# Six PSUM banks for scores, seven visits of three passes, relu on VectorE: a fused sigmoid attention and ReGLU kernel

## The chip, the cores and the metric

The kernel runs on one core of one Trainium2 chip. The time is device microseconds (us) of one launch; a run's profile gives a span that is some 2 us shorter.

TensorE is called PE, VectorE DVE, ScalarE ACT and GpSimd POOL, as the profile does.

## The reference

```python
# q, k, v: (8, 12, 448, 64)   batch, heads, seq, head_dim
scores = q @ k.T / sqrt(64) - log(448)
attn   = sigmoid(scores)                    # no softmax: no row sum is needed
o      = attn @ v
x      = o.transpose(0, 2, 1, 3).reshape(3584, 768)
gate   = maximum(x @ w_gate, 0)             # w_gate, w_val: (768, 1536)
val    = x @ w_val
out    = (gate * val) @ w_out               # w_out: (1536, 768)
```

## The kernel before

The work of a batch (448 rows) is attention on 12 heads, in three *blocks* of four heads, and then the feed-forward on 768 columns. A block has seven *passes*: a pass makes the scores of 64 key positions for four heads with four 64x64 matmuls, and one sigmoid of 896 columns on ACT. After a block's passes, 28 *value* matmuls make x^T for it, which is copied out of PSUM. (PSUM is where this kernel's matmuls put their results; it is divided into eight banks of 512 fp32 columns, and each is held by a tile from a pool until another engine has copied it out.)

The feed-forward of batch b runs on PE in 128x128 tiling. Into it are put *visits*: short interruptions in 64x64 tiling that do some passes, and sometimes the values, of batch b+1. Only the *opening* (batch 0's attention, some 30 us) has no feed-forward to hide it. Block n is head group n mod 3 of batch n // 3, so blocks 0 to 2 are the opening and blocks 3 to 5 are visited during batch 0's feed-forward.

```python
qkp = tile_pool("qkp", bufs=2, PSUM)        # 2 score tiles [128, 2, 512] fp32: 2 banks each
wkp = tile_pool("wkp", bufs=4, PSUM)        # 4 banks: gate, value, y, x^T, transposes

def scores(n, c):
    ps = qkp.tile([P, 2, 512], FP32)
    for r, h, o, bank in (...):             # four 64x64 quarters
        nc.tensor.matmul(ps[o:o+64, bank, 0:S], kT[...], qT[...], tile_position=(r, o), ...)
    nc.scalar.activation(pt, ps[:, :, 0:S], AF.Sigmoid, bias=bias_t, scale=qk_scale)

def up(b, f):                               # one 128-wide chunk of d_ff
    # 6 matmuls -> gate (wkp), relu on ACT; 6 matmuls -> value (wkp); product on DVE
    nc.scalar.activation(g_sb, acc[:, 0:S], AF.Relu)
    nc.vector.tensor_tensor(hT[f][...], g_sb, ps[1][:, 0:S], op=mult)

def visit():
    i0 = state["pass"]; n, c = divmod(i0, NCH)
    i1 = min(i0 + (3 if c == 0 and n > NBLK else 2), i0 + NCH - c, NPASS)
    for i in range(i0, i1):
        if c == 0 and i == i0 + 2 and n > NBLK:
            values(n - 1, range(NCH))
        scores(*divmod(i, NCH))
    ...                                     # then feed(i): loads, casts, transposes

# [cut]  the opening
for i in range(NP0 + 2):                    # NP0 = 21 passes
    scores(n, c)                            # while i < NP0
    ...                                     # values trail by 4 passes, later by 2
    if c == 1: cast_qk(n + 1, "k", nc.vector); cast_qk(n + 1, "q", nc.vector)
    if c in (3, 5): transposes(n + 1, "k" if c == 3 else "q")
    if 13 <= i < NP0: start_next()          # next load of weights or of a block
```

## Time and profile before

| | before |
|---|---|
| device time, median of 4 runs | 434.88 us (434.75 to 435.08) |
| span of the profiled run | 432.7 us |
| PE busy | 97% |
| sigmoids of the opening | 7.27 to 26.70 us |
| first gate matmul of the second chunk | 29.70 us |
| first gate matmul of batch 1 | 81.14 us |
| first gate matmul of batch 7 | 386.03 us |

The last four rows are marks: the starts of certain instructions in the timeline, in us from the start of the span. Since PE is nearly always busy, the distance of two marks is the time of a stage, and stages add up to the span. Two more rows, from the page's groups (busy us in total, mean ns of one, idle time of the engine ahead of them), show the work that the change moves between engines:

```profile
L232 ACT ACTIVATE gate_sb<-gv_ps 128x448 f32<-128x448 f32 x96 | 52.3, 544 | 91.6 <-PE gv_ps L220 91.6
...
L204 DVE TENSOR_SCALAR xT<-pv_ps 128x448 f16<-128x448 f32 x48 | 27.7, 619 | 127.1 <-PE pv_ps L191 127.1
```

The relu costs ACT 544 ns, and a copy of the same shape costs DVE 619 ns: DVE is the slower of the two for it.

### The profile page before, as it was taken

What the parts mean: (1) busy time and instruction counts of PE and PEld (TensorE: products, weight loads), DVE (VectorE), ACT (ScalarE), POOL (GpSimd) and SP (SyncE); (2) the same over time, 40 slices, a digit from 0 to 9 for tenths busy, and PEclk for the clock granted to TensorE, in tenths of its full rate; (3) what the DMA queues carried; (4) which work ended last, traced back from release to release, by engine and by line L of the source; (5) the groups of instructions that cost most, each with busy time, mean ns of one, the idle gap of its engine ahead of it and who ended that gap; (6) DMA issues with size and microseconds to landing.
All of it is one profiled execution on the core that took longest, in us unless ns stands there. A gap on an engine that the chain in (4) does not pass through costs nothing.

```text
span 432.7 us, 7894 instructions
## 1 busy us (share of the span) xinstructions
PE 421.4 (97%) x3296; PEld 214.6 (50%) x3296; DVE 99.5 (23%) x168; ACT 235.4 (54%) x325; POOL 105.6 (24%) x139
## 2 busy tenths in 40 slices
PE   7789999999999999999999999999999999999996
PEld 3344455544555445544455445554455544455554
DVE  3432332132202222122211233023220232212210
ACT  5955656655556656555546555565555556532221
POOL 2687669222301403113021133013030100000000
PEclk9999999999999999999999999999999999999999
DMA  8999997891238920695217932299114320030014
GB/s 302 385 385 385 388 394 261 229 268 46 42 77 238 300 45 2 172 244 163 42 42 198 251 126 44 53 234 294 22 21 111 79 44 2 17 94 1 2 36 111
DMA packets 62516, 66.52 MB, mean 154 GB/s; under 512 B 33936, under 2 KB 52752, under 8 KB 62480
## 3 DMA queue, kind: packets, MB, share of 16 engines
q1 hardware_dynamic: 61232, 64.17, 50.8%
q10 hardware_dynamic: 1248, 1.84, 1.2%
q8 instruction: 26, 0.43, 0.4%
q14 instruction: 10, 0.08, 0.1%
HBM read 47.19 MB, written 11.01 MB: 134 GB/s over the span
## 4 chain that ended last, share of the span: by engine, by line
PE 86%; DMA 6%; ACT 3%; POOL 2%; issue 1%; DVE 1%; SPq 0%; DVEq 0%; POOLq 0%
PE gv_ps L220 47%; PE y_ps L252 25%; PE qk_ps L167 8%; PE pv_ps L191 6%; DMA st_wo<-in_moe_w_out_dram 5%; ACT PT L177 3%; DMA st_k<-in_k_dram 2%; POOL wo L137 1%; PE tr L153 0%; POOL wg L137 0%; DVE xT L204 0%; SPq L90 0%; DVE h16q L105 0%; POOL v L112 0%; POOL v L114 0%
## 5 line engine op out<-in xcount | busy, mean ns | idle before, releaser
L177 ACT ACTIVATE PT<-qk_ps,bias_t 128x896 f16<-128x896 f32 x168 | 158.1, 1011 | 58.5 <-PE qk_ps L167 58.5
L220 PE MATMUL gv_ps<-xT,wv 128*128 128x448 f16 x576 | 127.8, 353 | 0.0
L220 PE MATMUL gv_ps<-xT,wg 128*128 128x448 f16 x576 | 127.4, 353 | 0.2 <-DVE xT L204 0.2
L252 PE MATMUL y_ps<-wo,hT 128*128 128x512 f16 (+2 forms) x684 | 114.5, 323 | 0.4 <-POOL wo L137 0.4
L232 ACT ACTIVATE gate_sb<-gv_ps 128x448 f32<-128x448 f32 x96 | 52.3, 544 | 91.6 <-PE gv_ps L220 91.6
L235 DVE TENSOR_TENSOR hT<-gate_sb,gv_ps 128x448 f16<-128x448 f32 x96 | 59.6, 621 | 168.1 <-PE gv_ps L220 137.5
L252 PEld LDWEIGHTS <-hT 128*128 128x128 f16 x684 | 64.2, 98 | 48.6 <-issue 8.2
L220 PEld LDWEIGHTS <-wv 128*128 128x128 f16 x576 | 54.6, 98 | 57.3 <-issue 8.6
L220 PEld LDWEIGHTS <-wg 128*128 128x128 f16 x576 | 54.9, 98 | 53.5 <-issue 5.7
L112 POOL CAST v<-st_v 128x448 f16<-128x448 f32 x24 | 13.5, 562 | 180.4 <-PE pv_ps L191 171.1
L204 DVE TENSOR_SCALAR xT<-pv_ps 128x448 f16<-128x448 f32 x48 | 27.7, 619 | 127.1 <-PE pv_ps L191 127.1
L167 PE MATMUL qk_ps<-qT,kT 64*64 64x448 f16 x672 | 51.4, 360 | 4.7 <-ACT PT L177 3.9
L264 ACT ACTIVATE ysb<-y_ps 128x512 f32<-128x512 f32 (+2 forms) x56 | 27.4, 489 | 39.8 <-PE y_ps L252 39.5
L191 PE MATMUL pv_ps<-PT,v 64*64 64x448 f16 x672 | 39.0, 349 | 0.8 <-ACT PT L177 0.8
L167 PEld LDWEIGHTS <-kT 64*64 64x64 f16 x672 | 15.4, 105 | 34.7 <-issue 30.1
L105 POOL CAST h16q<-st_q 128x896 f16<-128x896 f32 x21 | 19.6, 932 | 40.2 <-DMA kT<-h16k 32.8
L191 PEld LDWEIGHTS <-v 64*64 64x64 f16 x672 | 20.0, 107 | 12.6 <-issue 1.8
L105 POOL CAST h16k<-st_k 128x896 f16<-128x896 f32 x21 | 19.6, 932 | 0.4 <-DMA qT<-h16q 0.3
L114 POOL CAST v<-st_v 64x448 f16<-64x448 f32 x24 | 13.7, 570 | 1.0
L113 POOL CAST v<-st_v 64x448 f16<-64x448 f32 x24 | 13.4, 560 | 1.5
L137 POOL CAST wv<-st_wu 128x1536 f16<-128x1536 f32 x6 | 8.8, 1470 | 3.4 <-DMA st_wu<-in_moe_w_val_dram 3.4
L137 POOL CAST wg<-st_wg 128x1536 f16<-128x1536 f32 x6 | 8.8, 1467 | 2.0 <-DMA st_wg<-in_moe_w_gate_dram 1.7
(25 smaller groups left out, 47.9 us busy)
## 6 DMA issues: line engine op xcount, KB each, us to landing
out_dram<-ysb SPq DMA_DIRECT2D x54, 192.0 KB, 2.7
st_q<-in_q_dram SPq DMA_DIRECT2D x23, 448.0 KB, 5.9
st_v<-in_v_dram SPq DMA_DIRECT2D x23, 448.0 KB, 6.6
st_k<-in_k_dram SPq DMA_DIRECT2D x22, 448.0 KB, 5.0
st_wg<-in_moe_w_gate_dram SPq DMA_DIRECT2D x6, 768.0 KB, 12.2
st_wu<-in_moe_w_val_dram SPq DMA_DIRECT2D x6, 768.0 KB, 12.2
st_wo<-in_moe_w_out_dram SPq DMA_DIRECT2D x6, 768.0 KB, 11.4
st_v<-in_v_dram ACTq DMA_DIRECT2D x1, 448.0 KB, 5.4
```

The source lines that it names most:

```text
L105: eng.tensor_copy(o, i)
L114: eng.tensor_copy(t[64:128, 1], st[0:64, 1])
L137: eng.tensor_copy(dst, st[:])
L167: nc.tensor.matmul(ps[o : o + 64, bank, 0:S], kT[r : r + 64, c, h, :], qT[r : r + 64, :, h, :], start=True, stop=True, tile_position=(r, o ...
L177: nc.scalar.activation(pt[:], ps[:, :, 0:S], AF.Sigmoid, bias=bias_t[:], scale=qk_scale)
L191: nc.tensor.matmul(pv[pr][o : o + 64, 0:S], t[r : r + 64, pr, c * D : (c + 1) * D], pt[r : r + 64, pr, :], start=(c == 0), stop=(c == NCH ...
L204: nc.vector.tensor_scalar(out=x[:], in0=pv[pr][:, 0:S], scalar1=XSCALE, scalar2=None, op0=AOP.mult)
L220: nc.tensor.matmul(acc[:, 0:S], w[:, dc, jj * P : (jj + 1) * P], xT[b, dc][:], start=(dc == 0), stop=(dc == NDC - 1),)
L232: nc.scalar.activation(g_sb[:], acc[:, 0:S], AF.Relu)
L235: nc.vector.tensor_tensor(out=hT[f][:, o : o + S], in0=g_sb[:], in1=ps[1][:, 0:S], op=AOP.mult)
L252: nc.tensor.matmul(y[:, 0:w], hT[f][:, o : o + P], wo[f // FG][:, f % FG, c0 : c0 + w], start=(f == 0), stop=(f == NFC - 1),)
L264: nc.scalar.activation(dst, y[:, 0:w], AF.Copy, scale=OUT_SCALE)
```

## The change

The intent: fewer and larger visits. A visit of three passes needs three score tiles, six of the eight banks; the feed-forward is left with two, and so its banks must be freed fast. ACT would be in the way there, since its sigmoids come in threes; so relu and the output copies go to DVE, and the x^T copies to ACT. Block 3's transposes move into the opening, those of blocks 4 and 5 and the values go to score tiles, and those of block 6 to the DMA.

```diff
-    qkp = ... bufs=2, PSUM        wkp = ... bufs=4, PSUM
+    qkp = ... bufs=3, PSUM        wkp = ... bufs=2, PSUM
@@ transposes
+        if n <= NBLK: tr = wkp.tile(...)
+        else:         tr = qkp.tile([P, 2, 512], FP32, tag="qk")[:, 0, 0:S].bitcast(FP16) ...
@@ values
-            PT[n] = [wkp.tile([P, 512], FP32, tag="wk") for _ in range(2)]
+            PT[n] = qkp.tile([P, 2, 512], FP32, tag="qk")
-                nc.vector.tensor_scalar(out=x[:], in0=pv[pr][:, 0:S], scalar1=XSCALE, ... mult)
+                if n >= NBLK or (pr and n == NBLK - 1):
+                    nc.scalar.activation(x[:], pv[:, pr, 0:S], AF.Copy, scale=XSCALE)
+                else:
+                    nc.vector.tensor_scalar(...)
@@ up
-                nc.scalar.activation(g_sb[:], acc[:, 0:S], AF.Relu)
+        nc.vector.tensor_scalar(out=g_sb[:], in0=gate[:, 0:S], scalar1=0.0, ... max)
@@ down
-                if j == 0:                 # output copy on ACT
+                if nb == 2 and j == 0:     # only one of the two last, narrow ones
@@ feed: block m's transposes, while the block before it has its passes
-        if c == 0 and NPRO <= n + 3 < NB: load_all(n + 3)
-        if c == 4 and NPRO < m < NB: dma_transposes(m)
-        if c == 5 and NBLK < m <= NPRO: transposes(m, "k"); transposes(m, "q")
+        if c == 4 and NBLK < m < NPRO: transposes(m, "k"); transposes(m, "q")
+        if c == 3 and NPRO <= m < NB: dma_transposes(m)
+        if c == 3 and NPRO <= m + 1 < NB: load_all(m + 1)
@@ visit
-        i1 = min(i0 + (3 if c == 0 and n > NBLK else 2), i0 + NCH - c, NPASS)
+        i1 = min(i0 + 3, NPASS)            # may run over the end of a block
@@ the opening
-        order = halves("g", 0) + halves("u", 0) + [3] + ...
+        order = halves("g", 0) + [3] + halves("u", 0) + ...
+            if i == 14: cast_qk(NBLK, "k", nc.vector)
+            if i == 15: transposes(NBLK, "k"); cast_qk(NBLK, "q", nc.vector)
+            if i == 16: transposes(NBLK, "q")
+            if i in (18, 21): gv_part(0, 0, wg, [0, 1] if i == 18 else [2, 3])
@@ batches
-                count = 3 * NBLK + (2 if b == 0 else 0)          # 11, then 9
+                count = NBLK * NCH // 3 + (1 if b == 0 else 0)   # 8, then 7
-                if b == 0 and step == 12: transposes(NBLK, "k"); transposes(NBLK, "q")
# [cut: helpers for starting the first chunk's gate and value early, a set of blocks already valued,
#  how many loads are issued first, where batch 0's visits begin]
```

More of the change, by code (lines that the diff above doesn't have):

```diff
@@ L58 @@
     ysbp = ctx.enter_context(tc.tile_pool(name="ysbp", bufs=3))
-    qkp = ctx.enter_context(tc.tile_pool(name="qkp", bufs=2, space=bass.MemoryType.PSUM))
-    wkp = ctx.enter_context(tc.tile_pool(name="wkp", bufs=4, space=bass.MemoryType.PSUM))
+    qkp = ctx.enter_context(tc.tile_pool(name="qkp", bufs=3, space=bass.MemoryType.PSUM))
+    wkp = ctx.enter_context(tc.tile_pool(name="wkp", bufs=2, space=bass.MemoryType.PSUM))
     bias_t = const.tile([P, 1], FP32, name="bias_t")
@@ L150, in transposes @@
         h16 = qk16.pop((nm, n))
-        tr = wkp.tile([P, NCH, 2, KC], FP16, tag="wk", name="tr")
+        if n <= NBLK:
+            tr = wkp.tile([P, NCH, 2, KC], FP16, tag="wk", name="tr")
+        else:
+            tr = qkp.tile([P, 2, 512], FP32, tag="qk", name="tr")[:, 0, 0 : S].bitcast(FP16)
+            tr = tr.rearrange("p (c h k) -> p c h k", c=NCH, h=2)
         for c in range(cut[0], cut[-1]):
@@ L184, in values @@
         if chunks[0] == 0:
-            PT[n] = [wkp.tile([P, 512], FP32, tag="wk", name="pv_ps") for _ in range(2)]
+            PT[n] = qkp.tile([P, 2, 512], FP32, tag="qk", name="pv_ps")
         pv = PT[n]
@@ L191, in values @@
                 nc.tensor.matmul(
-                    pv[pr][o : o + 64, 0:S],
+                    pv[o : o + 64, pr, 0:S],
                     t[r : r + 64, pr, c * D : (c + 1) * D],
@@ L203, in values @@
                 x = xTp.tile([P, S], FP16, tag="xT", name="xT")
-                nc.vector.tensor_scalar(
-                    out=x[:], in0=pv[pr][:, 0:S], scalar1=XSCALE, scalar2=None, op0=AOP.mult
-                )
+                if n >= NBLK or (pr and n == NBLK - 1):
+                    nc.scalar.activation(x[:], pv[:, pr, 0:S], AF.Copy, scale=XSCALE)
+                else:
+                    nc.vector.tensor_scalar(
+                        out=x[:], in0=pv[:, pr, 0:S], scalar1=XSCALE, scalar2=None, op0=AOP.mult
+                    )
                 xT[b, 2 * i + pr] = x
@@ L212, with gv_part, up @@
     MM_US = 0.189
-    def up(b: int, f: int):
-        j, jj = divmod(f, FG)
-        ps = []
-        for w in (wg[j], wv[j]):
-            acc = wkp.tile([P, 512], FP32, tag="wk", name="gv_ps")
-            for dc in range(NDC):
-                nc.tensor.matmul(
-                    acc[:, 0:S],
-                    w[:, dc, jj * P : (jj + 1) * P],
-                    xT[b, dc][:],
-                    start=(dc == 0),
-                    stop=(dc == NDC - 1),
-                )
-                if dc < NDC - 1:
-                    yield MM_US
-            ps.append(acc)
-            if len(ps) == 1:
-                g_sb = gsbp.tile([P, S], FP32, tag="gsb", name="gate_sb")
-                nc.scalar.activation(g_sb[:], acc[:, 0:S], AF.Relu)
+    begun: dict = {}
+    def gv_part(b: int, f: int, w, dcs):
+        key = (b, f, w is wg)
+        if key not in begun:
+            begun[key] = wkp.tile([P, 512], FP32, tag="wk", name="gv_ps")
+        j, jj = divmod(f, FG)
+        for dc in dcs:
+            nc.tensor.matmul(
+                begun[key][:, 0:S],
+                w[j][:, dc, jj * P : (jj + 1) * P],
+                xT[b, dc][:],
+                start=(dc == 0),
+                stop=(dc == NDC - 1),
+            )
+        return begun[key]
+    def up(b: int, f: int, gate_done=0, val_first=0):
+        if val_first:
+            gv_part(b, f, wv, range(val_first))
+        for dc in range(gate_done, NDC):
+            gate = gv_part(b, f, wg, [dc])
+            if dc < NDC - 1:
+                yield MM_US
+        g_sb = gsbp.tile([P, S], FP32, tag="gsb", name="gate_sb")
+        nc.vector.tensor_scalar(out=g_sb[:], in0=gate[:, 0:S], scalar1=0.0, scalar2=None, op0=AOP.max)
+        yield MM_US
+        for dc in range(val_first, NDC):
+            val = gv_part(b, f, wv, [dc])
+            if dc < NDC - 1:
                 yield MM_US
         o = (b % NHALF) * S
-        nc.vector.tensor_tensor(
-            out=hT[f][:, o : o + S], in0=g_sb[:], in1=ps[1][:, 0:S], op=AOP.mult
-        )
+        nc.vector.tensor_tensor(out=hT[f][:, o : o + S], in0=g_sb[:], in1=val[:, 0:S], op=AOP.mult)
         yield MM_US
@@ L280, in ffn @@
         for f in range(NFC):
-            yield from up(b, f)
+            if b == 0 and f == 0:
+                yield from up(b, f, 4, 4)
+            else:
+                yield from up(b, f)
         for col0 in blocks128(b):
@@ L286, in ffn_us @@
         return NFC * 2 * NDC * MM_US + len(blocks128(b)) * NFC * (DM / 2400.0 + 0.004)
-    LOAD_AHEAD = 3
     NPRO = 2 * NBLK
@@ L299, in feed @@
         n, c = divmod(i, NCH)
-        m = n + LOAD_AHEAD
-        if c == 0 and NPRO <= m < NB:
-            load_all(m)
         m = n + 1
@@ L305, in feed @@
             cast_block(m)
-        if c == 4 and NPRO < m < NB:
-            dma_transposes(m)
-        if c == 5 and NBLK < m <= NPRO:
+        if c == 4 and NBLK < m < NPRO:
             transposes(m, "k")
             transposes(m, "q")
+        if c == 3 and NPRO <= m < NB:
+            dma_transposes(m)
+        if c == 3 and NPRO <= m + 1 < NB:
+            load_all(m + 1)
+    valued: set = set()
     state = {"pass": NBLK * NCH}
@@ L315, in visit @@
         i0 = state["pass"]
-        n, c = divmod(i0, NCH)
-        i1 = min(i0 + (3 if c == 0 and n > NBLK else 2), i0 + NCH - c, NPASS)
+        i1 = min(i0 + 3, NPASS)
+        n = i0 // NCH - 1
+        ready = n >= NBLK and n not in valued
         for i in range(i0, i1):
-            if c == 0 and i == i0 + 2 and n > NBLK:
-                values(n - 1, range(NCH))
+            if ready and i == i0 + 2:
+                values(n, range(NCH))
             scores(*divmod(i, NCH))
-        if i0 == NPASS:
-            values(n - 1, range(NCH))
+        if ready and i0 == NPASS:
+            values(n, range(NCH))
+        if ready:
+            valued.add(n)
         for i in range(i0, i1):
@@ L349, in halves @@
             return [(kind, j, 0), (kind, j, 1)]
-        order = halves("g", 0) + halves("u", 0) + [3] + halves("g", 1) + halves("u", 1)
+        order = halves("g", 0) + [3] + halves("u", 0) + halves("g", 1) + halves("u", 1)
         order += [4] + halves("g", 2) + halves("u", 2) + halves("o", 0) + [5]
@@ L358, in start_next @@
                 load_all(what)
-                cast_block(what)
+                if what > NBLK:
+                    cast_block(what)
+                else:
+                    cast_v(what, nc.gpsimd)
             else:
@@ L375 @@
             cast_v(n, nc.gpsimd)
-        for _ in range(4):
+        for _ in range(2):
             start_next()
@@ L398 @@
                 transposes(n + 1, "k" if c == 3 else "q")
-            if 13 <= i < NP0:
+            if i == 14:
+                cast_qk(NBLK, "k", nc.vector)
+            if i == 15:
+                transposes(NBLK, "k")
+                cast_qk(NBLK, "q", nc.vector)
+            if i == 16:
+                transposes(NBLK, "q")
+            if i in (18, 21):
+                gv_part(0, 0, wg, [0, 1] if i == 18 else [2, 3])
+            if 11 <= i < NP0:
                 start_next()
@@ L405 @@
             if b + 1 < B:
-                count = 3 * NBLK + (2 if b == 0 else 0)
-                lo = 4.0 if b == 0 else 0.0
+                count = NBLK * NCH // 3 + (1 if b == 0 else 0)
+                lo = 6.0 if b == 0 else 0.0
                 todo = [lo + (k + 0.5) * (total - lo) / count for k in range(count)]
@@ L411 @@
                 t += cost
-                if b == 0 and step == 12:
-                    transposes(NBLK, "k")
-                    transposes(NBLK, "q")
                 if order and step % 8 == 0:
```

## The prediction

> **What bounds the kernel now.** I read the page first: the busy line, then the 40 slices.
>
> ```profile
> PE 421.4 (97%) x3296; PEld 214.6 (50%) x3296; DVE 99.5 (23%) x168; ACT 235.4 (54%) x325; POOL 105.6 (24%) x139
> ...
> PE   7789999999999999999999999999999999999996
> ```
>
> PE is idle only in the first three slices and the last one. ACT, at 54%, is the next engine. So PE's own work sets the end; a change pays if it takes time out of PE's stream, or shortens the opening. A busy PE still need not be at its peak, so I looked in the timeline at how closely its matmuls follow each other.
>
> ```profile
> 100.37 0.92 PE L220 MATMUL gv_ps<-xT,wg 128*128 128x448 f16 x4
> ...
> 101.22 0.57 PE L167 MATMUL qk_ps<-qT,kT 64*64 64x448 f16 x8
> 101.66 1.91 ACT L177 ACTIVATE PT<-qk_ps,bias_t 128x896 f16<-128x896 f32 x2 [1.68 <-PE qk_ps L167]
> 101.73 0.55 PE L220 MATMUL gv_ps<-xT,wg 128*128 128x448 f16 x2
> ```
>
> Columns: start, duration, engine, line, instruction, count. Elsewhere six 448-wide matmuls start 1.135 us apart as a group (389.44 to 390.57 below), so one is 0.189 us. The four at 100.37 have streamed by 101.13; the feed-forward goes on at 101.73. The visit of two score passes thus takes 0.60 us. Its matmuls need 2 x 448/2.4 GHz = 0.373 us, the four 64x64 quarters running together. **0.23 us of each visit is the switch into and out of the 64x64 tiling.** A visit of three passes and 28 value matmuls (start 94.37; feed-forward from 94.28 to 96.39) takes 2.11 us against 10 x 0.187 = 1.87: 0.24 us again. The price is per visit, not per pass.
>
> Second, the buffers: how close is an evacuation to what PE needs next? In the last batch, which has no visits:
>
> ```profile
> 389.44 1.30 PE L220 MATMUL gv_ps<-xT,wv 128*128 128x448 f16 x6
> ...
> 390.57 1.30 PE L220 MATMUL gv_ps<-xT,wg 128*128 128x448 f16 x6
> 390.85 0.62 DVE L235 TENSOR_TENSOR hT<-gate_sb,gv_ps 128x448 f16<-128x448 f32 x1 [1.65 <-PE gv_ps L220]
> 391.71 1.30 PE L220 MATMUL gv_ps<-xT,wv 128*128 128x448 f16 x6
> ```
>
> The product starts 0.28 us after its group has streamed and ends at 391.47, 0.24 us before PE would want the same bank if there were two.
>
> Third, the opening and batch 0:
>
> ```profile
> 11.32 15.38 ACT L177 ACTIVATE PT<-qk_ps,bias_t 128x896 f16<-128x896 f32 x17 [0.35 <-PE qk_ps L167]
> ```
> ```profile
> 23.59 1.47 POOL L137 CAST wv<-st_wu 128x1536 f16<-128x1536 f32 x1 [0.57 <-DMA st_wu<-in_moe_w_val_dram]
> ...
> 26.09 0.94 POOL L105 CAST h16q<-st_q 128x896 f16<-128x896 f32 x1 [1.02 <-DMA st_q<-in_q_dram]
> ...
> 65.96 1.47 POOL L137 CAST wo<-st_wo 128x1536 f16<-128x1536 f32 x1 [0.51 <-DMA st_wo<-in_moe_w_out_dram]
> ...
> 67.48 1.79 PE L252 MATMUL y_ps<-wo,hT 128*128 128x512 f16 x13 [0.44 <-POOL wo L137]
> ```
>
> From 11.3 to 26.7 us ACT is gapless: 17 sigmoids at 0.905 us set the pace. The DMA moves 385 GB/s in the slices up to about 65 us; POOL casts wait for loads (brackets), and once PE waits 0.44 us for the last of w_out.
>
> **What the Trainium skill says.** "TensorEngine Tiling (Array Packing)", Key Properties: changing the tiling mode drains TensorE. The trace agrees: 0.23 us per visit. "TensorE: Matmul & The Clock Gate", Back-to-back issue gap: N/2.4 + 2.5 ns, for 448 columns 189.2 ns; the trace has 0.189 us. "VectorE: DVE Perf Modes", Mode 2x_2P: that mode needs SBUF, as PSUM has one read port; so I take relu on VectorE at the plain rate, like the present x^T copy (619 ns for 448 columns). "Perfetto Trace Analysis", Matmuls: groups should rotate through PSUM banks so that evacuation overlaps the next group; the change leaves just two for that.
>
> **The change part by part.**
>
> *Visits.* Batch 0 goes from 11 visits to 8, batches 1 to 6 from 9 to 7: 3 + 12 = 15 fewer. Passes and values stay the same. With three score tiles a visit's three passes need not wait for a sigmoid (visits are some 7 us apart, three sigmoids take 2.8). Gain 15 x 0.23 = **3.45 us** (2.76 in batches 1 to 6).
>
> *Relu and output copies to VectorE, x^T to ScalarE.* Neither is on PE's path. VectorE gets 2 x 0.62 us per 2.27 us of gate and value, 55%. What matters is the release: 0.28 + 0.62 us plus about 0.05 for the semaphore (an x^T copy ended at 28.33 and PE started at 28.38) = 0.95 us against 1.135 us until PE returns to that bank. Slack 0.19 us. For outputs: 0.3 + about 0.69 (152 ns + 512/0.96 GHz, estimated from the 619 ns copy) + 0.05 = 1.04 against 12 x 0.109 = 1.31 us. Slack 0.27. So **0**. ScalarE gains 2 x 0.54 us in three visits per batch: hidden.
>
> *Transposes on PE.* The 14 of one block take 0.79 us (42.13 to 42.92). Block 3's move into the ScalarE-paced opening, block 6's go to the DMA: gain **1.6 us**. Those of blocks 4 and 5 stay, but now write score tiles just after three passes have filled all three. The instruction order confirms that both wait for ScalarE. Take V as the start of a visit: sigmoids start at V + 0.44 and each 0.905 later, each lasting some 0.97. Block 4: k^T waits to V + 1.45 instead of 0.65, then q^T to V + 2.35: 1.3 us lost. Block 5's visit has values too: k^T waits 0.35 us and q^T, which takes the values' tile, 0.55 us for the x^T copies on ScalarE: 0.9. Loss **2.2 us**.
>
> *Loads.* Block 6's loads (1.38 MB, 3.6 us at 385 GB/s) move behind w_out, which lands that much earlier: the 0.44 us wait goes, gain **0.44 us**.
>
> *Opening.* Block 3 now loads ahead of w_val's first quarter. From the casts above, q of block 3 lands at about 19.5 + 2 x 1.2 = 21.9 instead of 26.1, and w_val 3.6 us later: its second half at about 27.2, cast by 28.7. PE transposes q of block 3 at pass 16, about 23.4 after the cast, some 1.1 us after pass 17's scores would have gone, so ScalarE's chain ends about 1.1 us later, near 27.9. The four gate matmuls done early, the split x^T copy and four early value matmuls should have won some 1.1 us; they now cover this delay. Gate and value of the first chunk end about together at 29.6, and the next gate waits for relu to about 30.15. Before, it started at 29.70. Loss **0.45 us**.
>
> *Sum.* 3.45 + 1.6 + 0.44 - 2.2 - 0.45 = 2.84 us. I take 3.2, since the early opening steps could hide more than I give them: 434.99 - 3.2 = **431.8 us**.
>
> **The rivals.**
>
> 1. *Two banks are too few.* If VectorE's release is later than I read by more than 0.19 us, PE stalls at nearly all 192 gate and value groups. At 0.05 us each that is 9.6 us and the time about 441. For it: the slack is small, and end times of pipelined matmuls are modelled. Against it: the 0.28 us lag repeats to 0.01 through the last batch, the product's mean of 621 ns holds while POOL works too, and ScalarE's sigmoids no longer delay relu. I give it one chance in ten in some degree.
>
> 2. *DMA transposes come too late.* They are now issued before a block's first pass by a margin of only one visit for some blocks. The pair before, issued at 135.83, released POOL at 140.2 and 141.5: 5.65 us. A gap between visits is at least 5.55 + 0.8 = 6.35 us. At the start of each batch I count k and q landing at 7.7 us and needed at 9.3. If that fails by 1 us in six batches the gain is gone: 438.
>
> 3. *The opening or the loads gain more.* If block 3's data come in time, the ScalarE chain keeps its 26.7 us end and some 1 us more is won; without the transposes' waits another 2.2 us: 428.5. Against it: at 385 GB/s nothing lands sooner, and three tiles are full when the transposes want them.
>
> More than 2% (8.7 us) is nowhere to be found: all visits' switches together were 65 x 0.23 = 15 us, and 50 remain.
>
> **Range and chances.** The visits' gain is firm, from a price that repeats; the other terms nearly cancel and are good to about 2 us. Down to 429.0 if rival 3 comes half true; up to 435.5 for a small stall of rivals 1 or 2. Faster by over 2%: 0.04. Slower by over 2%: 0.05. Within 2%: 0.91.
>
> **What the changed profile would show.** Right: a batch of 50.91 us (half of 84.27 to 186.09, two batches) becomes about 50.45; visits of three passes take about 0.79 us; gate groups still follow at 1.135 us and no wait of gv_ps for relu or product adds up, except in batch 0; tr waits for PT and x^T, some 2 us in total; no wait for w_out; the first chunk ends near 30 us. Wrong: gv_ps waiting for VectorE in every batch (rival 1), qk_ps waiting for kT or qT from the DMA (rival 2), or ScalarE's sigmoids of the opening ending away from 27.9 us. If a visit of three passes cost more than 0.79 us, the price would not be per visit and the main term would fall.

## The result, and the profile after

| | before | after |
|---|---|---|
| median of 4 runs each, us | 434.88 | 433.76 |
| lowest to highest, us | 434.75 to 435.08 | 433.40 to 434.29 |
| ratio after / before | | 0.9975 [0.9957, 0.9992] |

A ratio is the mean time of one kernel's fast runs over that of the other's of the same rounds, so it is not quite the ratio of the medians. The change gained 1.1 us, where 3.2 were forecast. The page of the changed kernel:

```profile
PE 418.7 (97%) x3282; PEld 216.6 (50%) x3282; DVE 165.9 (38%) x276; ACT 178.8 (41%) x217; POOL 102.6 (24%) x137
...
PE   7779899999999999999999999999999999999996
...
L230 PE MATMUL gv_ps<-xT,wg 128*128 128x448 f16 x576 | 128.1, 353 | 0.6 <-DVE gate_sb L247 0.3
...
L247 DVE TENSOR_SCALAR gate_sb<-gv_ps 128x448 f32<-128x448 f32 x96 | 59.9, 624 | 71.9 <-PE gv_ps L230 71.9
```

PE's busy time fell by 2.7 us, yet the span fell by just 0.2. Against the slices before, the third (21.6 to 32.4 us, the opening) and the fifth (43 to 54 us) each lost a tenth: time went missing early. The gate matmuls waited 0.6 us in the whole run, so two banks hardly stall the feed-forward.

The marks put the difference into stages. The predicted column takes the terms of the prediction that belong to a stage; for the rest of batch 0 those are three visits (-0.69), the transposes (-1.6 and +2.2) and w_out (-0.44).

| stage | before, us | after, us | change | predicted |
|---|---|---|---|---|
| start to the second chunk's first gate matmul | 29.70 | 32.17 | +2.47 | +0.45 |
| rest of batch 0 | 51.44 | 50.83 | -0.61 | -0.53 |
| batches 1 to 6 | 304.89 | 302.13 | **-2.76** | -2.76 |
| batch 7 to the end | 46.67 | 47.37 | +0.70 | 0 |
| span | 432.7 | 432.5 | -0.20 | -2.84 |

The profiled run of the changed kernel was its slowest (434.29 us, 0.53 above the median), so its opening is a bad one. In three more profiles of kernels with the same opening, in the experiments below, the first mark lay at 31.32, 31.66 and 32.96 us: the opening lost between 1.6 and 3.3 us. From the medians it is about 1.55: the other stages gained 0.61 + 2.76 - 0.70 = 2.67, and 1.12 arrived. (The other stages hardly vary: where an experiment leaves them alone, its profile has 50.8, 302.1 and 47.4 us for them again.)

**A visit of three passes** in the timeline (columns: start, duration, engine, line, operation, count; all times in us):

```profile
92.88 0.35 PE L230 MATMUL gv_ps<-xT,wg 128*128 128x448 f16 x1
...
93.16 0.76 PE L171 MATMUL qk_ps<-qT,kT 64*64 64x448 f16 x12
...
93.86 1.12 PE L230 MATMUL gv_ps<-xT,wg 128*128 128x448 f16 x5
```

The one gate matmul has streamed (its columns are all in) by 92.88 + 0.189 = 93.07, and the feed-forward goes on at 93.86. The visit takes 0.79 us for 3 x 0.187 us of matmuls: the price is 0.23 us, as it was for two passes.

**The opening's sigmoids** (timeline of ACT; the bracket is the idle time before a row and what ended it):

```profile
7.94 3.70 ACT L181 ACTIVATE PT<-qk_ps,bias_t 128x896 f16<-128x896 f32 x4 [0.49 <-PE qk_ps L171]
11.99 10.93 ACT L181 ACTIVATE PT<-qk_ps,bias_t 128x896 f16<-128x896 f32 x12 [0.35 <-PE qk_ps L171]
23.11 1.01 ACT L181 ACTIVATE PT<-qk_ps,bias_t 128x896 f16<-128x896 f32 x1 [0.19 <-PE qk_ps L171]
24.92 1.01 ACT L181 ACTIVATE PT<-qk_ps,bias_t 128x896 f16<-128x896 f32 x1 [0.81 <-PE qk_ps L171]
26.47 2.90 ACT L181 ACTIVATE PT<-qk_ps,bias_t 128x896 f16<-128x896 f32 x3 [0.54 <-PE qk_ps L171]
...
30.51 0.54 ACT L209 ACTIVATE xT<-pv_ps 128x448 f16<-128x448 f32 x1 [1.14 <-DVE xT L211]
```

Before, 17 sigmoids ran without a gap to 26.70. Now there are three gaps after 22.9 us and the last sigmoid ends at 29.37, 2.67 later. Counted in starts, at 0.905 us from one to the next: 0.67 is there from the first sigmoid on (7.94, before 7.27), the next two gaps delay the chain by 0.26 and 0.90, the last by 0.64. PE's side of the gaps:

```profile
11.07 0.55 PE L157 MATMUL tr<-ident,h16k 128*128 128x128 f16 x7 [1.48 <-DVE kT L163]
...
22.11 0.56 PE L157 MATMUL tr<-ident,h16k 128*128 128x128 f16 x7 [0.37 <-DVE h16k L105]
...
23.93 0.57 PE L157 MATMUL tr<-ident,h16q 128*128 128x128 f16 x7 [0.75 <-DVE h16q L105]
...
25.98 0.38 PE L171 MATMUL qk_ps<-qT,kT 64*64 64x448 f16 x4 [0.60 <-ACT PT L181]
...
32.17 1.29 PE L230 MATMUL gv_ps<-xT,wg 128*128 128x448 f16 x6 [0.34 <-DVE gate_sb L247]
```

Four things are to be seen. At 11.07 PE waits for one of the two feed-forward banks, whose k^T copy stands on DVE behind block 1's casts, which wait for their load. At 22.11 and 23.93 PE takes up block 3's transposes before their casts are done, and the next scores stand behind them. At 25.98 scores wait for a score tile: the values of block 2 hold one of the three. At 32.17 the second chunk's gate waits for the first chunk's relu.

The late start is in part luck. PE's first seven transposes, from 5.43 us, took 0.95 us here and 0.61 before, but between 0.60 and 0.95 from profile to profile of the edited kernels whose transposes start at that moment. Where they took 0.60 (e3_two), the first sigmoid started at 7.48, still 0.21 later than before.

**The end.** The last pair of output tiles, before (first fence) and after:

```profile
423.77 5.29 PE L252 MATMUL y_ps<-wo,hT 128*128 128x256 f16 x47
```
```profile
426.87 0.69 DVE L283 TENSOR_SCALAR ysb<-y_ps 128x512 f32<-128x512 f32 x1 [2.17 <-PE y_ps L269]
427.61 1.45 PE L269 MATMUL y_ps<-wo,hT 128*128 128x128 f16 x23 [0.73 <-DVE ysb L283]
```

The last block's columns 512 to 767 are made as two tiles of 128 columns at once, so with the 512-wide tile three banks are in use. Two exist: PE waits 0.73 us for the 512-wide copy.

### The profile page after: what moved, and what is told of

Same layout as the page of the kernel before. It is cut to its first block, busy times and chain, and to the rows that moved or that the text cites. A ratio compares the mean times of both kernels' runs of the same rounds, so it can differ in the third digit from the quotient of the medians.

```text
span 432.5 us, 7873 instructions
## 1 busy us (share of the span) xinstructions
PE 418.7 (97%) x3282; PEld 216.6 (50%) x3282; DVE 165.9 (38%) x276; ACT 178.8 (41%) x217; POOL 102.6 (24%) x137
## 4 chain that ended last, share of the span: by engine, by line
PE 93%; DMA 3%; ACT 2%; DVE 1%; issue 1%; ACTq 0%
PE gv_ps L230 51%; PE y_ps L269 26%; PE qk_ps L171 8%; PE pv_ps L195 6%; DMA st_k<-in_k_dram 3%; ACT PT L181 2%; PE fill L357 1%; PE tr L157 1%; ACT xT L209 0%; DVE ysb L283 0%; DVE h16k L105 0%; DVE xT L211 0%; DVE gate_sb L247 0%; DVE h16q L105 0%; ACT kT L161 0%
## 5 line engine op out<-in xcount | busy, mean ns | idle before, releaser
L247 DVE TENSOR_SCALAR gate_sb<-gv_ps 128x448 f32<-128x448 f32 x96 | 59.9, 624 | 71.9 <-PE gv_ps L230 71.9
L283 DVE TENSOR_SCALAR ysb<-y_ps 128x512 f32<-128x512 f32 (+2 forms) x56 | 31.1, 556 | 105.7 <-PE y_ps L269 105.7
L105 POOL CAST h16q<-st_q 128x896 f16<-128x896 f32 x20 | 18.6, 930 | 223.2 <-DMA st_q<-in_q_dram 199.5
L171 PE MATMUL qk_ps<-qT,kT 64*64 64x448 f16 x672 | 48.5, 359 | 2.4 <-ACT PT L181 2.1
L171 PEld LDWEIGHTS <-kT 64*64 64x64 f16 x672 | 16.2, 105 | 27.9 <-issue 21.7
L209 ACT ACTIVATE xT<-pv_ps 128x448 f16<-128x448 f32 x43 | 21.0, 547 | 6.0 <-PE pv_ps L195 4.8
L105 POOL CAST h16k<-st_k 128x896 f16<-128x896 f32 x20 | 18.6, 928 | 0.0
```

What stands on the lines that cost most here:

```text
L105: eng.tensor_copy(o, i)
L171: nc.tensor.matmul(ps[o : o + 64, bank, 0:S], kT[r : r + 64, c, h, :], qT[r : r + 64, :, h, :], start=True, stop=True, tile_position=(r, o ...
L209: nc.scalar.activation(x[:], pv[:, pr, 0:S], AF.Copy, scale=XSCALE)
L247: nc.vector.tensor_scalar(out=g_sb[:], in0=gate[:, 0:S], scalar1=0.0, scalar2=None, op0=AOP.max)
L283: nc.vector.tensor_scalar(out=dst, in0=y[:, 0:w], scalar1=OUT_SCALE, scalar2=None, op0=AOP.mult)
```

## The experiments

Each is an edit of the changed kernel. Times are medians; "before" is the kernel before in the same rounds. All are shown with the expectation ahead of the run. All outputs are right. Since "before" itself moves by up to 0.4 us, differences of 0.2 us to the changed kernel mean little.

| run | us (lowest to highest, runs) | ratio to before [95%] |
|---|---|---|
| e1_tail | 433.88 (432.81 to 435.08, 6) | 0.9974 [0.9957, 0.9990] |
| e2_opening | 433.88 (433.70 to 434.68, 5) | 0.9978 [0.9966, 0.9990] |
| e3_two | 438.35 (438.22 to 439.13, 4) | 1.0080 [1.0067, 1.0093] |
| e4_later | 431.78 (431.49 to 432.25, 5) | 0.9929 [0.9916, 0.9941] |
| o1_dve_order | 433.54 (433.47 to 433.68, 4) | 0.9965 [0.9950, 0.9980] |
| o2_values_later | 433.20 (432.56 to 434.56, 4) | 0.9960 [0.9931, 0.9988] |
| o3_opening | 432.06 (431.90 to 432.15, 4) | 0.9930 [0.9915, 0.9945] |
| e6_all | 429.16 (429.07 to 429.26, 4) | 0.9864 [0.9849, 0.9879] |
| e7_relu_scalar | 452.02 (451.57 to 453.05, 4) | 1.0389 [1.0368, 1.0410] |
| e8_four_banks | 464.14 (463.95 to 465.33, 4) | 1.0672 [1.0648, 1.0696] |
| e9_no_split | 434.08 (433.24 to 434.51, 4) | 0.9971 [0.9952, 0.9990] |

My theory after the first look: the visits gave what I said; the loss is in the opening, where too few buffers and late data starve ACT's chain, and in the end. The rivals: the visits gave less and something else made up for it; or the loss lies in the feed-forward with its two banks.

### Is the price per visit? (e3_two)

```diff
-        i1 = min(i0 + 3, NPASS)
+        i1 = min(i0 + 2, NPASS)             # 10 or 11 visits per batch, 12 in batch 0
-            if ready and i == i0 + 2:
+            if ready and i == i0 + 1:
```

> The changed kernel with visits of two score passes instead of three, so 25 more visits (batch 0: 12 for 8; later 62 for 41, besides one for values alone); everything else as it is. Theory A (each visit costs a fixed 0.22 to 0.23 us for the switch of tiling): 25 x 0.23 = 5.7 us more, about 439.5. Rival (the price is not per visit, or the visits' gain was given back by some wait): the time moves by less than 3 us.

It took 438.35 us, 4.6 more than the changed kernel. Batches 1 to 6 have 21 more visits (63 in place of 42) and took 306.98 in place of 302.13 us: 4.85 / 21 = 0.231 us each. Together with the 2.76 / 12 = 0.230 us of the change itself, this shows the price to be per visit, in both directions. The four more visits of batch 0 (0.92 us) did not show in that batch (50.79 against 50.83 us): transposes waited for ACT some 0.9 us less (0.96 us in two waits, against 1.83 in four), where just two tiles had been filled. That is most of why the time rose by 4.6 and not by the expected 5.7 us.

### The transposes' waits (e4_later)

Transposes of blocks 4 and 5 are done after 1.5 us of feed-forward, not at once after the visit:

```diff
-            transposes(m, "k"); transposes(m, "q")
+            held.append(m)
@@ batches
+                if held and t >= seen + 1.5:      # seen: t at the last visit
+                    m = held.pop(); transposes(m, "k"); transposes(m, "q")
```

> The changed kernel, but the PE transposes of blocks 4 and 5 run 1.5 us of feed-forward work after their visit instead of right at its end, when all three score tiles still wait for ScalarE. Theory A: the four waits of the transposes that the profile shows (0.79, 0.35, 0.37 and 0.32 us) go, the time falls by about 1.8 us to 432.0. Rival (batch 0 is paced by the loads of w_out): the waits go but PE waits for w_out instead and the time falls by less than 0.7 us.

It took 431.78 us, 2.0 less than the changed kernel. The waits, in the changed kernel (first fence) and here:

```profile
46.15 0.55 PE L157 MATMUL tr<-ident,h16k 128*128 128x128 f16 x7 [0.79 <-ACT PT L181]
...
47.05 0.55 PE L157 MATMUL tr<-ident,h16q 128*128 128x128 f16 x7 [0.35 <-ACT PT L181]
...
58.91 0.55 PE L157 MATMUL tr<-ident,h16k 128*128 128x128 f16 x7 [0.37 <-ACT PT L181]
...
59.78 0.55 PE L157 MATMUL tr<-ident,h16q 128*128 128x128 f16 x7 [0.32 <-ACT xT L209]
```
```profile
46.30 0.55 PE L157 MATMUL tr<-ident,h16k 128*128 128x128 f16 x7
46.69 0.55 PE L157 MATMUL tr<-ident,h16q 128*128 128x128 f16 x7
```

The brackets add up to 1.83 us of idle time, counted from the modelled ends of the matmuls ahead, which lie some 0.2 us after these have streamed. The rest of batch 0 fell from 50.83 to 48.61 us, by 2.22 us; the prediction had 2.2 us for these waits. So this loss was sized right, and it costs nothing to avoid.

### The last output tiles (e1_tail)

```diff
-            ys = [wkp.tile([P, 512], FP32, tag="wk") for _ in range(nb)]
+            if nb == 2: ys = [qkp.tile([P, 2, 512], FP32, tag="qk")[:, 0] for _ in range(nb)]
+            else:       ys = [wkp.tile([P, 512], FP32, tag="wk")]
```

> The changed kernel, but the two 128-wide output tiles of the very last block come from the score pool (six banks, idle by then) instead of the two feed-forward banks. Theory A (part of the missing gain is a new wait at the end: two tiles wanted at once from a pool of two while the 512-wide copy still holds one): the wait of 0.73 us on the VectorE copy before the last output matmuls goes, the stretch from the last batch's first gate to the end falls from 47.2 to about 46.7 us, the time by 0.4 to 0.6 us to about 433.3. Rival (the end is set by the last output transfers anyway): the wait goes but the time stays at 433.8.

In the trace it did what was expected: from batch 7 to the end 432.6 - 385.93 = 46.67 us, as before the change, 0.70 less than after it. In the times nothing shows (433.88 us), because the six runs lie 2.3 us apart; the profiled one had its second chunk at 32.96 us, 0.79 later than in the changed kernel's profile. Its expectation of 0.4 to 0.6 us is thus not confirmed by the times. Taken alone, the timed result is inconclusive; with the opening mended (e6_all) the end is 427.3 - 380.60 = 46.70 us again and the sum closes.

### The opening: which cause?

Block 3 taken out of the opening altogether (old order of loads, casts on POOL, transposes in batch 0 as before):

```diff
-        if n <= NBLK: tr = wkp.tile(...)
+        if n < NBLK: tr = wkp.tile(...)            # block 3 into score tiles
-        order = halves("g", 0) + [3] + halves("u", 0) + ...
+        order = halves("g", 0) + halves("u", 0) + [3] + ...
-            if i == 14: ...   if i == 15: ...   if i == 16: ...
# [cut: block 3's casts go back to POOL, and the first loads to their old number and pace]
+                if b == 0 and step == 12: transposes(NBLK, "k"); transposes(NBLK, "q")
```

> The changed kernel with block 3 taken out of the opening: loads in the old order (both halves of the first w_val quarter ahead of block 3), block 3 cast on POOL and transposed early in batch 0, there into score tiles. Early gate and value matmuls, the split x^T copy and the pools stay. Theory A (most of the missing gain was lost in the opening, where transposing block 3 waits for its load and holds up the sigmoid chain and, through late x^T copies, the score tiles): the opening's sigmoids run gapless from about 12 to 27 us again, the second chunk's first gate starts near 29.7 us instead of 32.2, 14 transposes (0.8 us) come back in batch 0, and the time falls by 1.2 to 1.8 us to about 432.3. Rival (batch 0 is paced by the loads, so an earlier start is given back as a wait for w_out): the opening ends earlier but a wait for w_out or its cast appears, and the time stays within 0.4 us of 433.8.

It took 433.88 us: no gain, where I had expected more than 1 us. The first mark came at 30.99 (1.18 earlier), but the rest of batch 0 took 51.62 us, 0.79 more, which is the price of the 14 transposes there. And the chain of sigmoids still had gaps: 0.73 and 0.35 us ahead of the 5th and the 7th sigmoid, 0.54 ahead of the 19th. The first two follow a wait of 1.86 us for block 0's k^T copy, after which PE also ran slower for a while (the next seven q transposes took 0.93 us, in the changed kernel 0.56); what slowed it, no run here shows. For the third, PE's timeline:

```profile
23.91 0.57 PE L195 MATMUL pv_ps<-PT,v 64*64 64x448 f16 x8 [0.33 <-ACT PT L181]
24.80 0.38 PE L171 MATMUL qk_ps<-qT,kT 64*64 64x448 f16 x4 [0.32 <-ACT PT L181]
```

Scores at 23.01 were followed by the next only at 24.80, with no block 3 in sight: the start of block 2's values took the third score tile. Before the change, values had their own banks. So my theory of block 3 as *the* cause fell; the move to score tiles is a second one. It also bears on the loads: here block 3 loads in its old place, and still the last cast of w_out began at 62.56 us in place of 65.96, 3.4 us earlier, near the 3.6 us predicted for block 6's later load. (That PE did not wait for w_out shows less here, since PE came to it later, too. In e6_all below PE comes to it 0.87 us earlier than before the change, and doesn't wait either.)

Next the other causes, one at a time. Block 0's second k^T copy ahead of block 1's casts on DVE:

```diff
-            if c == 1 and n + 1 < NBLK:
+            if (c == 1 and 1 <= n < NBLK - 1) or i == 2:    # block 1's casts, after that copy
```

> The changed kernel; on VectorE the second k^T copy of block 0 now goes ahead of block 1's casts, which wait for their load. Nothing else. Theory A (the opening lost time in several small waits, one of which is new because only two feed-forward banks are left for the transposes and the filler): PE's wait for that copy before block 1's transposes (1.5 us in the changed kernel's profile, up to 2.9 in others) goes and the fifth sigmoid follows the fourth without the 0.35 us gap. Since block 3's loads hold the chain up later anyway, the time falls by only 0.2 to 0.6 us, to about 433.4, and the runs lie closer together. Rival (the opening's spread comes from the clock or the loads alone): no change in time or spread.

433.54 us, 0.2 less; but the four runs lie 0.2 us apart, where the changed kernel's lie 0.9. PE's wait of 1.48 us had cost ACT just 0.35 us (at 11.99), as much as ACT waited there before the change, but it hangs on when block 1's load lands: in the profile of e1_tail it was 2.9 us. In this run's profile the first 16 sigmoids have no gap, and then the 17th waits 1.01 us (0.19 in the changed kernel): PE takes up block 3's transposes before the cast of its k is done. What the early part had won was lost there. How much of the changed kernel's spread is due to it was not measured apart.

Block 2's first values at pass 19 in place of 17:

```diff
-            while done <= i - (4 if i < NP0 - 4 else 2):
+            while done <= {17: 13, 18: 13, 19: 16}.get(i, i - (4 if i < NP0 - 4 else 2)):
```

> The changed kernel; block 2's first values wait for pass 19 instead of coming at pass 17, so that block 1's values tile is free before block 2 takes one. Theory A (in the opening values and scores share three tiles; with two of them held by values only one is left for scores): PE's wait of 0.60 us before the 19th score pass and ScalarE's gap of 0.54 us go, the second chunk's first gate moves from about 32 to about 31.5 us, the time falls by 0.3 to 0.6 us. Rival (the gap comes from block 3's transposes): the gap stays and so does the time.

433.20 us, 0.56 less, with a range of 2 us; the wait of 0.60 us ahead of pass 18 is gone from its trace. Alone it is too uncertain to count on.

Both of these, and block 3's transposes two passes later, when their casts are done:

```diff
-            if i == 14: cast k      if i == 15: transpose k, cast q     if i == 16: transpose q
-            if i in (18, 21): gv_part(...)
+            if i == 15: cast k      if i == 16: cast q
+            if i in (17, 18): transposes(NBLK, "k" if i == 17 else "q")
+            if i in (20, 21): gv_part(...)
```

> The changed kernel with both of these, and with block 3's transposes two passes later, behind block 1's x^T copies on VectorE. Theory A (the opening lost about 1.5 us more than was predicted, by these waits): the 21 sigmoids run from about 7.3 to 26.5 us with no gap over 0.2 us except at the start, the second chunk's first gate starts at about 30.2 us, bound now by the cast of the second half of the first w_val quarter (29.3 us), and the time falls by 1.2 to 1.8 us to about 432.2. Rival (w_val's cast, not the sigmoid chain, sets the start): less than 0.6 us.

432.06 us, 1.7 less than the changed kernel, and the runs 0.25 us apart. ACT's timeline:

```profile
7.58 19.01 ACT L181 ACTIVATE PT<-qk_ps,bias_t 128x896 f16<-128x896 f32 x21 [0.49 <-PE qk_ps L171]
```

All 21 sigmoids now run without a gap, 19.01 / 21 = 0.905 us each, to 26.59 us. The first mark is at 29.93, 0.23 later than before the change. Part of what holds it there is a new wait, in PE's timeline:

```profile
28.47 0.36 PE L230 MATMUL gv_ps<-xT,wv 128*128 128x448 f16 x1 [0.60 <-POOL wv L137]
```

That is the cast of the second half of the first w_val quarter, which block 3 displaced in the order of loads. From the last sigmoid to the first mark it takes 3.34 us here, 0.54 more than in the changed kernel. How much of that is this wait was not tested.

Last, the split copy of x^T in the opening. One of block 2's two copies was given to ACT so that they run together, but in the trace ACT's begins at 30.51, just after DVE's ended (29.85 + 0.62 = 30.47).

```diff
-                if n >= NBLK or (pr and n == NBLK - 1):
+                if n >= NBLK:                     # both of block 2's copies on DVE
```

> The changed kernel with both x^T copies of block 2 on VectorE, as before the change. Theory A (the copies on two engines run one after the other anyway, since both read one tile: the profile has ScalarE wait for VectorE's copy): the second gate matmul waits about as long, the time stays within 0.2 us of 433.7. Rival (the copies overlap on two engines): 0.5 us slower.

434.08 us against 433.76, with ranges that overlap; the first mark at 31.73. From the end of the last sigmoid to the first mark it took 2.76 us here and 2.80 with the split. The split gains nothing. The trace says why the two copies do not overlap: in its bracket ([1.14 <-DVE xT L211], shown above) ACT waits for a semaphore that DVE's copy sets. So the program orders the two, which read one score tile. Whether two tiles would let them overlap was not tried.

### Are the other parts needed? (e7_relu_scalar, e8_four_banks)

The relu alone back on ACT:

```diff
-        nc.vector.tensor_scalar(out=g_sb[:], in0=gate[:, 0:S], scalar1=0.0, ... max)
+        nc.scalar.activation(g_sb[:], gate[:, 0:S], AF.Relu)
```

> The changed kernel with only relu back on ScalarE (output copies and all else as changed). Theory A (with two feed-forward banks a bank must come free within 1.135 us, and relu must therefore not queue behind a visit's sigmoids): a gate group that ends soon after a visit finds relu behind up to three sigmoids and two x^T copies (to about 3.2 to 4.3 us after the visit's start), PE stalls 1 to 2 us after most of the 36 or so visits that fall in the gate and value stretches, the time rises by 30 to 60 us to 465 to 495. Rival (two banks are ample with either engine): less than 3 us slower.

452.02 us, 18.3 more. Its view of waits, PE's first line (total us, times, longest):

```profile
PE gv_ps L230 <- ACT gate_sb L247: 13.9, 15, 1.6
```

The direction was as expected, the size well short of the 30 to 60 us: there are 15 such stalls with 50 visits, not one with most of them. In one of them three sigmoids run on ACT from 96.51 to 99.31, the relu starts at 99.20 and PE goes on at 99.80 after 0.77 us of waiting. The kernel before has the relu on ACT too and four banks, and its waits have no such line.

The old split of banks, with all else as changed:

```diff
-    qkp bufs=3, wkp bufs=2;   values and transposes in qkp
+    qkp bufs=2, wkp bufs=4;   values and transposes in wkp
```

> The changed kernel with the old bank split: two score tiles (four banks) and four feed-forward banks, values and transposes in those; seven visits of three passes and all else as changed. Theory A (three passes per visit need a third score tile): in the 29 or so visits without values the third pass waits for the first sigmoid, from 0.37 to 1.45 us after the visit's start, 29 x 1.08 = 31 us lost, less 2.9 us for the waits of the transposes and of the last tiles, which go: about 462 us. Rival (the third tile isn't needed): about 431.

464.14 us, 30.4 more, near the expected 462. From its view of waits:

```profile
PE qk_ps L171 <- ACT PT L181: 30.9, 36, 1.0
```

The third pass of a visit waits for the first sigmoid. So with three passes in a visit, leaving out either the new split of banks or the move of relu makes the kernel slower than it was before the change; what either would do to the kernel before was not tried.

### All mended together (e6_all)

The edits of o3_opening, e4_later and e1_tail in one kernel.

> All corrections together: the opening as in the run before this one, the transposes of blocks 4 and 5 run 1.5 us of work after their visit (1.8 us measured), the last output tiles from the score pool (0.7 us of the final stretch measured). If these three are separate terms of one sum: 433.8 - 1.5 - 1.8 - 0.7 = 429.8 us, 1.2% under the kernel before. Rival (they overlap, or the loads of w_out pace batch 0): above 431.

**429.16 us: 5.7 us less than before, and faster than both kernels.** Against the kernel before by stages: the opening +0.15 (29.85 us), the rest of batch 0 -2.82 (48.62), batches 1 to 6 -2.76 (302.13), the end +0.03 (46.70): -5.40 in the span, 427.3 for 432.7. The expected sum was 429.8 us; the rival, that the three terms overlap, would have come out above 431. Rivals that put the loss into the feed-forward have nothing left to explain.

## Why the prediction was right or wrong

- **The visits, 3.45 us: right.** The twelve of batches 1 to 6 gave 2.76, the number of the prediction, and e3_two gave the same price the other way. Batch 0's three are in its sum only.
- **Relu and copies on VectorE, "So 0": right for the relu, wrong for the outputs.** Relu releases its bank 0.31 us before PE wants it (89.68 + 0.62 = 90.30, next gate at 90.61 in the trace), a little more than my 0.24 (0.19 once 0.05 for the semaphore is taken off), and takes 624 ns where I took 619. Rival 1 did not come. For the outputs I reckoned with tiles of 512 and 256 columns that take turns on two banks, and overlooked that the last block uses three tiles at once. This term was 0 in the sum and is 0.70 us; e1_tail took it away in the trace.
- **Transposes: right.** The rest of batch 0 was to gain 0.53 and gained 0.61; e4_later measured the waits alone, 2.22 for 2.2 (by the starts in its timeline and the changed kernel's some 1.4 for block 4 and 0.9 for block 5, against 1.3 and 0.9). Rival 2 (late DMA transposes) did not come: PE waits for no such transpose.
- **Loads, 0.44 us: consistent.** The wait for w_out is gone, and w_out comes as much earlier as I said; no run measured its worth by itself.
- **The opening, "Loss 0.45 us": the step that failed.** It was about 1.55 us by the medians and 2.47 in the profile. The mechanism, ACT's chain delayed by block 3's transposes, was right as far as it went. Two terms of its sum were not. First, "near 27.9" for the end of the chain: it was 29.37, and 28.5 to 30.2 in the three other profiles. I had counted block 3's delay of 1.1 us, which came (0.26 + 0.90), and taken the remaining chain as gapless. The values in a score tile (0.64) and the late start (0.67, of which some 0.5 looks like luck) were not in it. Second, the early matmuls and "the split x^T copy" that "should have won some 1.1 us". From the last sigmoid to the second chunk it took 29.70 - 26.70 = 3.00 us before and 32.17 - 29.37 = 2.80 after, and 2.79 to 2.80 in three other profiles: they won 0.2. (My sum had 30.15 - 27.9 = 2.25 us here, 0.55 too little.) The copies run one after the other, and the next gate still waits for relu. In the profile the two make 1.47 + 0.55 = 2.02 us, which is all of 2.47 - 0.45.
- **"I take 3.2":** I raised the sum of 2.84 because the early steps "could hide more". They hid less. This alone is 0.36 us of the miss.
- **Together:** of the 2.1 us between forecast and measured gain, 0.36 is that rounding up, 0.70 is the end, and 1.1 (1.55 - 0.45) the opening. The other terms were good to 0.1 us. The change stayed within 2%, as forecast.

Still open: how much each of the opening's causes is worth alone. The edits of o1 and o2 gave 0.2 and 0.6 us with ranges of up to 2 us, all three together 1.7.

## What to carry to other kernels

The switch of tiling on PE had a price per interruption (0.23 us here) and not per unit of work, so batch the interruptions, and pay for it with banks where another engine can free the rest in time. When a change takes banks from a pool, list every place where that pool holds its most tiles at once, the opening and the last tile above all: the steady state was right here to 0.1 us, and all that was lost beyond the forecast lay at the two ends. An instruction put into an engine's order a little before its data or its buffer is ready delays all behind it; moving such ones by a microsecond or two was worth 3.7 us here (1.7 in the opening, 2.0 for blocks 4 and 5), more than the change itself.

## What the Trainium skill lacked or had wrong

- "TensorEngine Tiling (Array Packing)", Key Properties, says that a change of mode drains TensorE, but not what it costs. Here it was 0.23 us for going from 128x128 to 64x64 and back, with two, three or ten passes' worth of work between: 2.76 us for 12 switches fewer, 4.85 us for 21 more.
- "Perfetto Trace Analysis", Optimizing Scalar/DVE Operations, gives an overhead of some 125 ns for DVE on PSUM as busy time, and about twice that as profiled latency. Output copies in the profile took 0.69 us for 512 columns and 0.29 for 128: 1.04 ns per column and a fixed 0.16 us (worked out from these two), between the two figures.
